# Planner with durations of the trace, fillers in any of four free banks, another front, and a table of shifts to the due dates

## The chip, the cores and the metric

The kernel runs on one core of one Trainium2 chip. What counts is the device time of one launch in microseconds (us). Before the change it is 611.71 us, the median of three runs (611.14 to 612.87).

The engines are TensorE (PE in the profile, with its weight loads as PEld), VectorE (DVE), ScalarE (ACT), GpSimd (POOL) and SyncE (SP, which only issues DMAs here). Each engine works through its own list of instructions in order. TensorE writes into eight accumulator banks, bank 0 to bank 7. In the order lists below these are called bank_63 to bank_70.

## The reference

Banded attention with a distance bias, and after it two feed-forward layers (FFN) of the same size, all in float32 with inputs of large spread:

```python
def _attn_ref(q, k, v, n_global, n_local):          # 2 x 8 heads x 768 x 64
    scores = scale * np.matmul(q, k.transpose(0, 1, 3, 2))
    is_global = pos[None, :] < int(n_global)         # 8
    is_local = (rel >= 0) & (rel < int(n_local))     # 96
    bias = -slopes[:, None, None] * dist[None, :, :]
    scores = np.where(keep, scores + bias, -1e9)
    a = np.exp(scores - np.max(scores, axis=-1, keepdims=True))
    a = a / (np.sum(a, axis=-1, keepdims=True) + 1e-09)
    return np.matmul(a, v)

def _moe_ref(x, w_in, w_out):                        # 1536 tokens, 512 -> 2048 -> 512
    h = np.maximum(x @ w_in, 0.0)
    return h * h @ w_out

def _moe2_ref(x, w_in, w_out):
    h = x @ w_in
    g = np.where(h >= 1, h, np.where(h <= -1, 0.0, (h + 1) ** 2 / 4))
    return g @ w_out
```

`reference` calls the three in this order.

## The kernel before

**Attention** is cut into 12 blocks of 128 queries (6 for each batch), and each block into two halves of four heads. One half runs through these steps: scores (TensorE, line 872, 4 or 8 products into two banks); a reduction with the mask for each head (VectorE, L894), which writes the scores plus bias back to SBUF and keeps the extreme of each row; the exponential for each head (ScalarE, L899); the sums' reciprocal (VectorE, L904 and L906); a scaling for each head (lines 155 to 159, on ScalarE, VectorE or GpSimd); transposes (TensorE, L922); a copy of the transposed part out of the bank (L131 on ScalarE or L132 on VectorE); and the products with v (TensorE, L958, "results" below). A block ends with its column of `x`, split in two float32r parts: a copy (L131 or L132) and a subtraction (L142). The masks are made once at the start, from `n_global` and `n_local`, which a small product (`broadcast_int64`, L1173) spreads over all partitions.

**Layer 0 of the FFN** is a list of 52 events (`Ffn.__init__`). An event is one 128-wide chunk of the hidden layer for 256 or 512 tokens: twelve products `h` (L537), the square of the positive part (L552 on ScalarE, L554 on VectorE), its split in two parts (L131 and L142 with output `g`), and twelve products `y` (L735) into banks 2 to 5. The first eight events are 256 tokens wide and need the first four blocks of the attention; so the attention's later blocks and the first events run between each other. Events are numbered from 0 here. An event needs the weights of its chunk in a slot: they come as raw words (`float32`, L464), ScalarE scales them (L155), VectorE puts the bits together in three passes (L472, L475, L479), and both split them into the slot's parts (L131, L142). Layer 1 works on pairs of chunks (L654 and L704).

**What sets the order.** No engine's list is written out by hand. Every operation goes to `Plan.any_of` with its engines, an assumed duration on each, a due date and the tiles that it reads and writes. `Plan.emit` then simulates the engines: whenever one is free it takes, among the operations whose inputs are ready by the assumed durations, the one that is due first, and a copy or a scaling goes to the engine of its list that would end it earlier. The program's lists are what comes out. `BEGIN`, `OTHER`, `ns_mm`, `ns_turns` and their like are the assumed times. None of them runs on the chip.

**Warm products.** The eight products of L1348 at the start multiply a tile of zeros into bank 7. Further ones, 256 columns wide, are put in where the planner sees TensorE without work for over 300 ns (`FGAP`): into bank 7 while that bank isn't used yet (L1351), later into the upper half of bank 0 (L1353), up to the first event that is 512 wide. Their results are never read.

Of the kernel before, what the change touches and what calls it, by code (L numbers as in the profile page):

```python
# [37 lines left out]
WARM, LAG = 8, 950  # L38


FGAP, BIAS = 300, 600
# [16 lines left out]
HINTED = [E.Pool, E.Activation, E.PE, E.DVE, E.SP]  # L58
BIG = 1e30
MASKED = 1e9  # L60
TOP = 3e38
P = 128
# [11 lines left out]
class Plan:  # L74
# [14 lines left out]
    def __init__(self, nc):  # L89
        self.nc = nc  # L90
        self.ops = []
        self.wrote = {}
        self.read = {}


        self.idle = []

        self.sums = {}

        self.before = {}  # L100

# [3 lines left out]
    def any_of(self, ways, due, reads=(), writes=(), lag=0, rows=P, same=SAME, tail=False):  # L105
# [5 lines left out]
        deps = set()  # L111
        writes = list(writes)
# [38 lines left out]
    def scale(self, n, due, out, in_, by, reads, writes, engines=None):  # L151
# [3 lines left out]
            ("act", ns_act(n) + (0 if isinstance(by, float) else 107), lambda: nc.scalar.activation(  # L155
# [8 lines left out]
    def emit(self):  # L164
# [35 lines left out]
        fills, idle = [], list(self.idle)  # L200
        last, open_sums, port = 0, False, 0.0
        todo = n
        while todo:
# [52 lines left out]
            if idle and i >= idle[0][2] and idle[0][1] in ops[i][5]:  # L256
                idle.pop(0)
            if engine == "pe" and idle and not open_sums:

                gap, at = t - free[engine], free[engine]  # L260
                if gap > FGAP:
                    cold = 1 + (columns.get(int(t / self.TICK) - 1, 0) < self.COLUMNS)
                    one = cold * ns_mm(256)
                    for _ in range(int((gap - 150) / one)):
                        fills.append((at, 1, idle[0][0]))
# [16 lines left out]
            free[engine] = t + ns  # L282
            todo -= 1
# [11 lines left out]
def ns_mm(n, m=P):  # L295
    return max(n, 2 * m) * 0.442 + 4


def ns_turns(n):

    return (n + 1) * 110 + 280
# [10 lines left out]
def ns_pool(n):  # L312
    return n / 0.44 + 60
# [7 lines left out]
class Ffn:  # L321
# [108 lines left out]
    def make_after(self, u):  # L430

        while self.makes and self.makes[0][1] <= u:
# [5 lines left out]
            else:  # L438
                self.make(key, i, e["due"])

# [83 lines left out]
    def h(self, u):  # L524
# [24 lines left out]
        due += 0.4 * e["len"] - G_LEAD  # L549
        bank = ("bank", kb)  # L550
# [7 lines left out]
        self.halves(N, due, r, kr, g, kg)  # L558
        self.g[u] = kg, g
# [68 lines left out]
    def pair(self, u, past):  # L628
# [12 lines left out]
        def product(kb, name, w, half, blocks, m=None, sums=True):  # L641
# [14 lines left out]
            op("pe", len(calls) * ns_mm(W), start + step[name], products, reads, [("bank", kb ^ odd)])  # L656
# [39 lines left out]
    def pair_y(self, u, n, t, due):  # L696
# [6 lines left out]
        for m, (a, b) in enumerate(MOVING):  # L703
            self.plan.op("pe", ns_mm(512), due + 0.01 * m, lambda a=a, b=b, m=m: self.nc.tensor.matmul(  # L704
# [60 lines left out]
    def leave(self, o, bank, r0, due, end):  # L765
# [690 lines left out]
```

## Time and profile before

| | before |
|---|---|
| median of the runs | 611.71 us |
| the profiled execution, its own time | 612.07 us |
| its span in the trace | 610.2 us |
| TensorE busy, share of the span | 599.0 us, 98% |
| VectorE busy | 480.0 us, 79% |
| ScalarE busy | 351.2 us, 58% |
| GpSimd busy | 60.1 us, 10% |
| granted TensorE clock, mean | 0.998 |

The span is what lies between the first and the last instruction of the program; the 1.9 us beside it are the launch's own. "Busy" counts the warm products too. The ends of the records of TensorE are modelled and reach over the next record's start, so that its steps are read from one start to the next. The records of the other engines also overlap a little with the record that follows.

### The profile page before, as it was taken

What the parts mean: (1) busy time and instruction counts of PE and PEld (TensorE: products, weight loads), DVE (VectorE), ACT (ScalarE), POOL (GpSimd) and SP (SyncE); (2) the same over time, 40 slices, a digit from 0 to 9 for tenths busy, and PEclk for the clock granted to TensorE, in tenths of its full rate; (3) what the DMA queues carried; (4) which work ended last, traced back from release to release, by engine and by line L of the source; (5) the groups of instructions that cost most, each with busy time, mean ns of one, the idle gap of its engine ahead of it and who ended that gap; (6) DMA issues with size and microseconds to landing.
All of it is one profiled execution on the core that took longest, in us unless ns stands there. A gap on an engine that the chain in (4) does not pass through costs nothing.

```text
span 610.2 us, 9671 instructions
## 1 busy us (share of the span) xinstructions
PE 599.0 (98%) x3438; PEld 513.5 (84%) x3438; DVE 480.0 (79%) x1028; ACT 351.2 (58%) x728; POOL 60.1 (10%) x88
## 2 busy tenths in 40 slices
PE   7999999999999999999999999999999999999996
PEld 5778978887888888888888898999988888999995
DVE  7999999974638987898556379999897688887863
ACT  7898877765537766564447465454543454454432
POOL 4120111010000204226200000000000000000000
PEclk9999999999999999999999999999999999999999
DMA  8553544430013879989522211323230032222002
GB/s 301 172 183 119 181 153 143 157 126 23 20 54 107 278 215 327 338 308 308 201 83 70 65 56 58 108 77 102 73 99 31 12 127 96 95 96 95 27 2 106
DMA packets 25786, 79.20 MB, mean 130 GB/s; under 512 B 2948, under 2 KB 2948, under 8 KB 25732
## 3 DMA queue, kind: packets, MB, share of 16 engines
q1 hardware_dynamic: 25730, 78.52, 38.4%
q8 instruction: 28, 0.46, 0.3%
q14 instruction: 26, 0.21, 0.1%
q10 hardware_dynamic: 2, 0.00, 0.0%
HBM read 62.78 MB, written 15.73 MB: 129 GB/s over the span
## 4 chain that ended last, share of the span: by engine, by line
PE 94%; ACT 2%; DMA 2%; DVE 1%; issue 0%; DVEq 0%; ACTq 0%
PE bank L704 22%; PE bank L735 21%; PE bank L537 21%; PE bank L654 19%; PE bank L958 3%; PE bank L922 3%; PE bank L872 3%; ACT pr L899 1%; DMA nat<-in_v_dram 1%; DMA raw<-in_moe_w_out_dram 1%; PE bank L1348 0%; PE bank L1353 0%; ACT m L155 0%; DVE x L142 0%; ACT whole L155 0%
## 5 line engine op out<-in xcount | busy, mean ns | idle before, releaser
L660 DVE TENSOR_TENSOR pr<-bank,pr 128x384 f32<-128x384 f32 x112 | 60.2, 553 | 23.8 <-PE bank L654 23.0
L142 DVE TENSOR_TENSOR g<-r,g 128x512 fp32r<-128x512 f32 (+2 forms) x74 | 49.0, 663 | 33.8 <-ACT g L131 32.8
L552 ACT ACTIVATE r<-bank 128x512 f32<-128x512 f32 (+1 forms) x52 | 29.2, 562 | 55.2 <-PE bank L537 55.0
L131 ACT ACTIVATE g<-r 128x512 fp32r<-128x512 f32 (+2 forms) x74 | 42.7, 577 | 25.3 <-DVE r L569 14.6
L899 ACT ACTIVATE pr<-pr,mn 128x256 f32<-128x256 f32 (+1 forms) x96 | 45.9, 481 | 4.4 <-DVE mn L894 4.1
L565 ACT ACTIVATE r<-pr,small 128x384 f32<-128x384 f32 x43 | 26.2, 615 | 33.9 <-DVE pr L660 33.9
L155 ACT ACTIVATE whole<-raw 128x512 f32<-128x512 f32 x52 | 34.0, 670 | 10.2 <-DMA raw<-in_moe_w_in_dram 4.0
L479 DVE SCALAR_TENSOR_TENSOR whole<-raw,whole 128x512 uint32<-128x512 uint32 x52 | 36.5, 709 | 0.4
L894 DVE CUSTOM_DVE_ANT_0 pr<-bank,m 128x256 f32<-128x256 f32 (+1 forms) x96 | 33.4, 396 | 4.3 <-PE bank L958 4.1
L475 DVE SCALAR_TENSOR_TENSOR whole<-raw,whole 128x512 uint32<-128x512 uint32 x52 | 35.4, 693 | 0.3
L159 POOL TENSOR_SCALAR pr<-pr,mn 128x256 f32<-128x256 f32 (+1 forms) x38 | 22.3, 597 | 120.0 <-DVE mn L906 56.3
L872 PEld LDWEIGHTS bank<-nat,nat 64*128 64x128 f32 x352 | 22.2, 187 | 7.6 <-issue 2.2
L567 DVE SCALAR_TENSOR_TENSOR r<-r 128x384 f32<-128x384 f32 x43 | 23.8, 556 | 5.9 <-ACT r L565 5.1
L872 PE MATMUL bank<-nat,nat 64*128 64x128 f32 x352 | 26.6, 285 | 1.7 <-DVE mn L894 1.6
L472 DVE TENSOR_SCALAR whole<-whole 128x512 uint32<-128x512 uint32 x52 | 23.5, 456 | 5.2 <-ACT whole L155 4.9
L565 ACT ACTIVATE nat<-pr,small 128x384 f32<-128x384 f32 x21 | 13.0, 617 | 25.0 <-DVE pr L660 24.9
L131 ACT ACTIVATE pr<-bank 128x512 f32<-128x512 f32 (+2 forms) x46 | 23.5, 520 | 3.9 <-PE bank L654 2.1
L958 PE MATMUL bank<-pr,nat 128*64 128x128 f32 x352 | 23.9, 277 | 1.4 <-DMA nat<-in_v_dram 0.8
L569 DVE TENSOR_TENSOR r<-pr,r 128x384 f32<-128x384 f32 x43 | 23.8, 557 | 1.2
L958 PEld LDWEIGHTS bank<-pr,nat 128*64 128x64 f32 x352 | 19.7, 136 | 5.5 <-issue 2.0
L922 PE MATMUL bank<-ident,pr 128*128 128x128 f32 x176 | 24.1, 275 | 0.0
L922 PEld LDWEIGHTS bank<-ident,pr 128*128 128x128 f32 x176 | 20.1, 140 | 3.0 <-issue 0.5
(349 smaller groups left out, 1752.3 us busy)
## 6 DMA issues: line engine op xcount, KB each, us to landing
raw<-in_moe_w_in_dram SPq DMA_DIRECT2D x32, 512.0 KB, 4.6
raw<-in_moe_w_out_dram SPq DMA_DIRECT2D x32, 512.0 KB, 4.9
whole<-sums SPq DMA_DIRECT2D x14, 512.0 KB, 3.2
kept<-whole SPq DMA_DIRECT2D x12, 512.0 KB, 6.2
whole<-kept SPq DMA_DIRECT2D x12, 512.0 KB, 3.3
whole<-kept SPq DMA_DIRECT2D x13, 384.0 KB, 2.9
sums<-pr SPq DMA_DIRECT2D x8, 512.0 KB, 6.3
nat<-in_k_dram SPq DMA_DIRECT2D x12, 256.0 KB, 3.3
```

The costliest lines, as they stand in the source:

```text
L131: ("act", ns_act(n) - 30 * psum, lambda: nc.scalar.activation(out=at(out), in_=in_, func=ACTF.Copy), False),
L142: ways = [("dve", ns_dve(n), lambda: nc.vector.tensor_tensor(out=at(out), in0=in_, in1=at(hi).bitcast(F32), op=ALU.subtract), not psum)]
L537: op("pe", ns_mm(N), due + 0.01 * m, lambda k=k, a=a, b=b, m=m: nc.tensor.matmul(out=hp, lhsT=sl[a][:, 0, k * P:(k + 1) * P], rhs=self.x[: ...
L565: op("act", ns_act(N) + 64, due, lambda: nc.scalar.activation(out=r, in_=h, func=ACTF.Relu, bias=self.half, scale=0.5), keys, [kr])
L654: nc.tensor.matmul(out=area[kb], lhsT=lhsT, rhs=at(rhs), start=(m == 0), stop=(m == len(calls) - 1))
L660: op("dve", ns_dve(W), start + step[name] + 0.2 - G_LEAD, lambda: nc.vector.tensor_tensor(out=to, in0=area[kb], in1=in1, op=ALU.add), [("b ...
L704: self.plan.op("pe", ns_mm(512), due + 0.01 * m, lambda a=a, b=b, m=m: self.nc.tensor.matmul(out=self.banks[kb], lhsT=g[:, a, cs], rhs=sel ...
L735: lambda o=o, lhsT=lhsT, rhs=rhs, n=n: nc.tensor.matmul(out=o, lhsT=lhsT, rhs=rhs, start=(e["first"] and n == 0), stop=(e["last"] and n == 2),
L872: nc.tensor.matmul(**c)
L899: op("act", ns_act(w) + 200, due, lambda e=e: nc.scalar.activation(out=pr[:, e, :w], in_=pr[:, e, :w], func=ACTF.Exp, bias=mn[:, e:e + 1], ...
L922: self.nc.tensor.transpose(self.banks[kbs[m]][:, o:o + P], pr[:, 2 * m + e, c * P:(c + 1) * P], self.ident)
L958: nc.tensor.matmul(**c)
```

## The change

It has five parts; the order in which the work goes to `Plan` is the same.

1. **Assumed times.** A product of n columns counts n / 2.4 + 13.3 ns instead of n x 0.442 + 4; groups of scores, transposes and results get formulas and lags of their own; engines begin at other times (`BEGIN`); a wait across from TensorE counts 199 ns instead of 260; a GpSimd subtraction n / 0.3 + 60 instead of n / 0.44 + 60; loads of q, k and v 1000 instead of 728.
2. **Fillers.** `idle` is now a table of four banks (7, 0, 1, 6). Where the planner sees a gap before the first wide event, it takes the bank that is clear first, by the end of the last reader of what was last written there.
3. **The front.** Five warm products at the first date and two at -9.5, instead of eight at the first. The loads of v of blocks 0 and 1 get a later date.
4. **A table `SHIFT`** of 134 numbers that are added to the due dates of whole groups: a half's scores and probabilities ("p"), its transposes and results ("r"), a block's loads ("q", "k", "v"), an event's weights ("w"), an event's square and split ("g"), and a preparation of kept weights ("prep").
5. **Output rows** that leave before the last group go out in two DMAs of 256 columns instead of one of 512.

```diff
-WARM, LAG = 8, 950
-FGAP, BIAS = 300, 600
+AGAIN = 2
+WARM, LAG = 5, 950
+FGAP, BIAS, CLEAR = 300, 600, 200
...
+SHIFT = {
+    ("g", 0): 0.83, ("g", 1): -0.13, ("g", 2): 2.01, ("g", 3): -0.22, ("g", 4): -8.66, ("g", 5): 3.04,
...
+    ("w", 9): 19.63, ("w", 10): 16.13, ("w", 11): -20.83, ("w", 28): -0.43, ("w", 29): 24.68, ("w", 30): 0.09,
...
-    OTHER = {"pe": 260, "act": 150, "dve": 130, "pool": 200}
-    BEGIN = {"act": 2000, "dma": 1680, "words": 1680, "pool": 1080, "dve": 630, "pe": 1120}
+    OTHER = {"pe": 199, "act": 150, "dve": 130, "pool": 200}
+    BEGIN = {"act": 2560, "dma": 1360, "words": 740, "pool": 1260, "dve": 980, "pe": 1390}
...
+        self.tags.append(self.tag)
+        due += SHIFT.get(self.tag, 0)
...
-            if idle and i >= idle[0][2] and idle[0][1] in ops[i][5]:
-                idle.pop(0)
-            if engine == "pe" and idle and not open_sums:
-                gap, at = t - free[engine], free[engine]
-                if gap > FGAP:
+            if engine == "pe" and not idle_end:
+                idle_end = i == self.wide
+            if engine == "pe" and idle and not idle_end and not open_sums and t - free[engine] > FGAP:
+                clear = {}
+                for bank in idle:
+                    w = wrote.get(bank)
+                    read = [u for u in users[w] if "pe" not in ops[u][0]] if w is not None else []
+                    if all(by[u] for u in read):
+                        clear[bank] = max([end[u] + CLEAR for u in read], default=0.0)
+                if clear:
+                    bank = min(clear, key=lambda b: (max(clear[b], free[engine]), -clear[b]))
+                    at = max(clear[bank], free[engine])
...
 def ns_mm(n, m=P):
-    return max(n, 2 * m) * 0.442 + 4
+    return max(n, 2 * m) / 2.4 + 13.3
 def ns_turns(n):
-    return (n + 1) * 110 + 280
+    return n * 109 + 320
+def ns_columns(n):
+    return n * 109 + 245
+def ns_transposes(n):
+    return n * 109 - 80
...
+                plan.op("dma", 364, due, lambda h=h: nc.sync.dma_start(
+                    out=self.out[r0:r0 + P, h], in_=ot[:, h]), [(*ko, n)], (), lag=LAG)
+            return
...
-            for c, lead in (("k", 3), ("q", 2.5), ("v", 2)):
+            for c, lead in (("k", 3), ("q", 2.5), ("v", 2 if blk > 1 else 0.3)):
...
-        for n in range(WARM):
-            plan.op("pe", ns_mm(512), -500 + n, lambda: nc.tensor.matmul(
+        for n in range(WARM + AGAIN):
+            plan.op("pe", ns_mm(512), -500 + n if n < WARM else -9.5, lambda: nc.tensor.matmul(
...
-        plan.idle = [[lambda: nc.tensor.matmul(
...
+        plan.idle = {("bank", kb): lambda kb=kb: nc.tensor.matmul(
+            out=banks[kb][:, 0:256], lhsT=warm[:, 0:P], rhs=warm[:, 0:256], start=True, stop=True,
+        ) for kb in (7, 0, 1, 6)}
```

Three places show what this makes of the engines' lists.

TensorE at the start, before. The product with `small` (L1173) is the broadcast of `n_global` and `n_local`; four more pairs like the first two rows stand ahead of this piece.

```order
L1348 LDWEIGHTS warm
L1348 MATMUL bank_70<-warm 128x512
L1348 LDWEIGHTS warm
L1348 MATMUL bank_70<-warm 128x512
L1173 MATMUL bank_69<-small,r_122 128x2
L1348 LDWEIGHTS warm
L1348 MATMUL bank_70<-warm 128x512
L1348 LDWEIGHTS warm
L1348 MATMUL bank_70<-warm 128x512
L872 MATMUL bank_63<-nat_125,nat_126 128x128
```

TensorE at the start, after the change (the broadcast is L1243, a warm product L1418, scores L936). One more pair like the first two rows stands ahead.

```order
L1418 LDWEIGHTS warm
L1418 MATMUL bank_70<-warm 128x512
L1418 LDWEIGHTS warm
L1418 MATMUL bank_70<-warm 128x512
L1243 MATMUL bank_69<-small,r_122 128x2
L1418 LDWEIGHTS warm
L1418 MATMUL bank_70<-warm 128x512
L1418 LDWEIGHTS warm
L1418 MATMUL bank_70<-warm 128x512
L1418 LDWEIGHTS warm
L1418 MATMUL bank_70<-warm 128x512
L936 MATMUL bank_65<-nat_125,nat_126 128x128
```

The broadcast stood behind six warm products and now stands behind three; in the first scores, those of block 0's second half are now ahead of those of its first half.

VectorE before the first event, before. L472, L475 and L479 are the three passes over a chunk's weights; `whole_118` holds chunk 0 and `whole_119` chunk 1; the subtraction into `x` ends block 1.

```order
L157 TENSOR_SCALAR pr<-pr,mn_77 128x256
L472 TENSOR_SCALAR whole_118<-whole_118 128x512 x2
L475 SCALAR_TENSOR_TENSOR whole_118<-raw_116,whole_118 128x512 x2
L479 SCALAR_TENSOR_TENSOR whole_118<-raw_116,whole_118 128x512
L472 TENSOR_SCALAR whole_119<-whole_119 128x512
L479 SCALAR_TENSOR_TENSOR whole_118<-raw_116,whole_118 128x512
L142 TENSOR_TENSOR slot0l<-whole_118,slot0h 128x512
L142 TENSOR_TENSOR x<-bank_69,x 128x4x128
L475 SCALAR_TENSOR_TENSOR whole_119<-raw_117,whole_119 128x512
```

VectorE there after the change (the passes are L527, L530 and L534, the subtractions L175, the scaling L190).

```order
L190 TENSOR_SCALAR pr<-pr,mn_77 128x256 x2
L534 SCALAR_TENSOR_TENSOR whole_119<-raw_117,whole_119 128x512
L175 TENSOR_TENSOR slot1l<-whole_119,slot1h 128x512
L527 TENSOR_SCALAR whole_118<-whole_118 128x512 x2
L530 SCALAR_TENSOR_TENSOR whole_118<-raw_116,whole_118 128x512
L175 TENSOR_TENSOR slot1l<-whole_119,slot1h 128x512
L534 SCALAR_TENSOR_TENSOR whole_118<-raw_116,whole_118 128x512
L175 TENSOR_TENSOR x<-bank_69,x 128x4x128
L530 SCALAR_TENSOR_TENSOR whole_118<-raw_116,whole_118 128x512
L175 TENSOR_TENSOR slot0l<-whole_118,slot0h 128x512
```

Chunk 1's weights are now whole before chunk 0's, and both stand ahead of the first `h`; before, chunk 1's came later.

TensorE at event 2, before: `h` is the product with `slot2`, into bank_63; the eight scores (L872) ahead of this piece belong to it too.

```order
L735 MATMUL bank_68<-g_121,slot1h 128x256
L872 MATMUL bank_69<-nat_125,nat_126 128x128
...
L958 MATMUL bank_64<-pr,nat_127 64x128 x8
L537 MATMUL bank_63<-x,slot2l 128x256
L922 MATMUL bank_69<-ident,pr 128x128 x4
L537 MATMUL bank_63<-x,slot2h 128x256
L922 MATMUL bank_70<-ident,pr 128x128 x4
L537 MATMUL bank_63<-x,slot2h 128x256
```

TensorE at event 2, after the change (`h` is L592, transposes L986).

```order
L592 MATMUL bank_63<-x,slot2h 128x256
L792 MATMUL bank_68<-g_121,slot1h 128x256
L792 MATMUL bank_68<-g_121,slot1l 128x256
L792 MATMUL bank_68<-g_121,slot1h 128x256
L986 MATMUL bank_69<-ident,pr 128x128 x4
L986 MATMUL bank_70<-ident,pr 128x128 x4
L592 MATMUL bank_63<-x,slot2l 128x256
L592 MATMUL bank_63<-x,slot2h 128x256 x2
```

Between event 1's last `y` and event 2's `h` there stood scores, results and transposes of two halves; now there are the transposes of one. Over the whole list before event 2's first `y`, TensorE had 64 scores, 48 transposes and 40 results, and now has 48, 32 and 32.

## Rows read from the trace of the kernel before

**Rows 1.** The page: the span, and TensorE's busy time.

```profile
span 610.2 us, 9671 instructions
PE 599.0 (98%) x3438; PEld 513.5 (84%) x3438; DVE 480.0 (79%) x1028; ACT 351.2 (58%) x728; POOL 60.1 (10%) x88
```

**Rows 2.** Stretches: length, each engine's busy us (instructions), clock, DMA share, GB/s.

```profile
0.00:20.00 20.00, 16.36 (x143) 11.66 (x145) 15.22 (x72) 15.45 (x53) 8.38 (x25) 1.00 0.69 250
20.00:60.00 40.00, 37.23 (x367) 32.17 (x366) 36.76 (x117) 33.70 (x96) 6.66 (x11) 1.00 0.53 170
60.00:180.00 120.00, 120.00 (x919) 99.70 (x918) 91.21 (x263) 78.98 (x211) 12.42 (x20) 1.00 0.33 109
605.40:610.20 4.80, 0.00 (x0) 0.00 (x0) 0.00 (x0) 0.60 (x1) 0.00 (x0) 0.81 0.31 115
```

**Rows 3.** Stretches again, warm products alone: PE, PEld, DVE.

```profile
4.80:20.00 15.20, 3.60 (x26) 2.51 (x25) 0.00 (x0) 1.00 0.75 281
20.00:60.00 40.00, 4.11 (x27) 2.38 (x27) 0.00 (x0) 1.00 0.53 170
60.00:610.20 550.20, 0.00 (x0) 0.00 (x0) 0.00 (x0) 1.00 0.37 122
```

**Rows 4.** Timeline of TensorE, first 8 us: start, us, what, [idle before, releaser].

```profile
1.47 2.74 PE L1348 MATMUL bank<-warm 128*128 128x512 bf16 x6 [1.47 <-DVE warm L1346]
4.01 0.38 PE L1173 MATMUL bank<-small,r 128*128 128x2 f32 x2
4.25 0.59 PE L1348 MATMUL bank<-warm 128*128 128x512 bf16 x2
4.77 1.16 PE L872 MATMUL bank<-nat,nat 64*128 64x128 f32 x16
7.73 0.49 PE L872 MATMUL bank<-nat,nat 64*128 64x128 f32 x4 [1.58 <-DVE mn L894]
```

**Rows 5.** Timeline of VectorE, 2 to 8 us.

```profile
2.46 0.15 DVE L1170 SCALAR_TENSOR_TENSOR small<-small,words 1x2 f32<-1x2 f32 x1
4.63 0.29 DVE L1008 TENSOR_SCALAR whole<-whole,bank 128x128 f32<-128x128 f32 x1 [2.02 <-ACT small L1175]
6.75 0.27 DVE L894 CUSTOM_DVE_ANT_0 pr<-bank,m 128x128 f32<-128x128 f32 x1
```

**Rows 6.** Chain of waits, 17 to 50 us: start, us, what.

```profile
21.45 4.72 DMA raw<-in_moe_w_out_dram
42.20 4.85 DMA nat<-in_v_dram
```

**Rows 7.** Timeline of TensorE: first `y` of events 2, 4 and 18.

```profile
45.87 0.39 PE L735 MATMUL bank<-g,slot2h 128*128 128x256 f32 x1
62.33 0.28 PE L735 MATMUL bank<-g,slot0h 128*128 128x256 f32 x1
174.37 0.39 PE L735 MATMUL bank<-g,slot1h 128*128 128x512 f32 x1
```

**Rows 8.** Steps of TensorE: timeline for 256 columns and transposes, chain for 512.

```profile
60.14 0.28 PE L537 MATMUL bank<-x,slot1l 128*128 128x256 f32 x1
60.26 0.40 PE L537 MATMUL bank<-x,slot1h 128*128 128x256 f32 x2
18.01 0.66 PE L922 MATMUL bank<-ident,pr 128*128 128x128 f32 x4
18.01 1.09 PE L922 MATMUL bank<-ident,pr 128*128 128x128 f32 x8
174.54 2.72 PE bank L735 x12
```

**Rows 9.** VectorE's groups by form, 0 to 60 us (busy, mean ns), and one timeline row.

```profile
L894 DVE CUSTOM_DVE_ANT_0 pr<-bank,m 128x256 f32<-128x256 f32 x35 | 13.1, 417 | 0.0
L132 DVE COPY pr<-bank 128x512 f32<-128x512 f32 x4 | 2.7, 684 | 0.7 <-PE bank L922 0.7
18.07 1.27 DVE L475 SCALAR_TENSOR_TENSOR whole<-raw,whole 128x512 uint32<-128x512 uint32 x2
```

More of the change, by code (lines that the diff above doesn't have):

```diff
@@ L93, in __init__ @@
         self.read = {}
-        self.idle = []
+        self.idle, self.wide = {}, 0
         self.sums = {}
         self.before = {}
+        self.tag = None
+        self.tags = []
     def op(self, engine, ns, due, fn, reads=(), writes=(), lag=0, rows=P, tail=False, port=False):
@@ L198, in stream @@
                 columns[int(t / self.TICK)] = columns.get(int(t / self.TICK), 0) + c
-        fills, idle = [], list(self.idle)
+        fills, idle, idle_end, wrote = [], self.idle, False, {}
         last, open_sums, port = 0, False, 0.0
@@ L255, in emit @@
                 continue
-            if idle and i >= idle[0][2] and idle[0][1] in ops[i][5]:
-                idle.pop(0)
-            if engine == "pe" and idle and not open_sums:
-                gap, at = t - free[engine], free[engine]
-                if gap > FGAP:
+            if engine == "pe" and not idle_end:
[10 more added lines that the diff above has]
+                    at = max(clear[bank], free[engine])
                     cold = 1 + (columns.get(int(t / self.TICK) - 1, 0) < self.COLUMNS)
                     one = cold * ns_mm(256)
-                    for _ in range(int((gap - 150) / one)):
-                        fills.append((at, 1, idle[0][0]))
+                    for _ in range(int((t - at - 150) / one)):
+                        fills.append((at, 1, idle[bank]))
                         stream(at, at + one, 256)
@@ L282, in emit @@
             free[engine] = t + ns
+            if engine == "pe":
+                for k in ops[i][5]:
+                    wrote[k] = i
             todo -= 1
@@ L312, in ns_pool @@
 def ns_pool(n):
-    return n / 0.44 + 60
+    return n / 0.3 + 60
 def ns_pool2(n):
@@ L654, in products @@
                     nc.tensor.matmul(out=area[kb], lhsT=lhsT, rhs=at(rhs), start=(m == 0), stop=(m == len(calls) - 1))
-            op("pe", len(calls) * ns_mm(W), start + step[name], products, reads, [("bank", kb ^ odd)])
+            op("pe", len(calls) * ns_mm(W) + 13, start + step[name], products, reads, [("bank", kb ^ odd)], lag=24)
         def add(name, kb, in1, k1, to, key):
@@ L874, in scores @@
         op("pe", ns_turns(len(calls)), due, products, [("q", rq, 0)] + [("k", rk, 0) for rk in self.rings(blk)],
-           [("bank", kb) for kb in kbs], rows=64)
+           [("bank", kb) for kb in kbs], lag=-97, rows=64)
     def probabilities(self, blk, j, due):
@@ L923, in transposes @@
                             self.banks[kbs[m]][:, o:o + P], pr[:, 2 * m + e, c * P:(c + 1) * P], self.ident)
-        self.plan.op("pe", 2 * nk * len(ms) * 108 + 80, due, transposes, [("pr", n % 3, 2 * m + e) for m in ms for e in range(2)],
-                     [("bank", kbs[m]) for m in ms], rows=64)
+        self.plan.op("pe", ns_transposes(2 * nk * len(ms)), due, transposes,
+                     [("pr", n % 3, 2 * m + e) for m in ms for e in range(2)], [("bank", kbs[m]) for m in ms], lag=83, rows=64)
         w = 2 * nk * P
@@ L958, in products @@
                 nc.tensor.matmul(**c)
-        op("pe", ns_turns(len(calls)), due, products, reads, [("bank", kb)], rows=P)
+        op("pe", ns_columns(len(calls)), due, products, reads, [("bank", kb)], lag=-98, rows=P)
         if 1 in js:
@@ L1162, in broadcast_int64 @@
     nc.vector.memset(ones, 1.0)
-    for n, (way, queue, src) in enumerate(zip(("words", "dma"), (nc.scalar, nc.sync), srcs)):
-        plan.op(way, 475, -300, lambda n=n, queue=queue, src=src: queue.dma_start(
+    for n, (way, ns, lag, queue, src) in enumerate((
+            ("words", 475, 775, nc.scalar, srcs[0]), ("dma", 50, 580, nc.sync, srcs[1]))):
+        plan.op(way, ns, -300, lambda n=n, queue=queue, src=src: queue.dma_start(
             out=words[0:1, 2 * n:2 * n + 2], in_=src.bitcast(I32).rearrange("(o n) -> o n", o=1),
-        ), (), [("words", n)], lag=960)
+        ), (), [("words", n)], lag=lag)
     low, high, r = words[0:1, 0:4:2], words[0:1, 1:4:2], one[0:1, 0:2]
@@ L1367 @@
             at.finish()
-            plan.idle[0][2] = len(plan.ops)
             at.use_banks([(6, 7)], [6, 7], [1], False)
```

27 lines of the change are left out of this document (19 added, 8 removed), and 21 rows, old and new, of the table SHIFT.

## The prediction

> **What bounds the kernel now.** I read the page first. TensorE is busy for 98% of the span [rows 1], so the time is TensorE's work, what is put between it, and what it waits. The stretches tell where the last two lie: from 60 us on TensorE is busy without a gap to the last product at 605.4, and the 4.8 us behind it hold copies and stores; in the first 60 us it is idle for 3.6 and 2.8 us [rows 2], and 3.60 and 4.11 us more are warm products between 4.8 and 60 us, none later [rows 3]. So only the front can give time back. The tail can't: the two order lists of TensorE agree from their ends back over more than a thousand products.
>
> In the front VectorE is the engine that TensorE waits for. Between 20 and 60 us it is busy for 36.8 of 40 us and ScalarE for 33.7 [rows 2]. The first gap ends on VectorE's reductions [rows 4]. The chain of waits runs twice through a DMA of 4.7 to 4.9 us, for an event's raw weights and for a block of v [rows 6].
>
> To measure how far TensorE lags I subtract its useful work from the clock at a landmark. Its steps: 0.40 - 0.28 = 0.12 us for 256 columns, 2.72 / 12 = 0.227 us for 512, (1.09 - 0.66) / 4 = 0.108 us for a score, transpose or result [rows 8]. Event 2's first `y` comes at 45.87, event 4's at 62.33, event 18's at 174.37 [rows 7]. Ahead of them the order lists hold:
> - event 2: 152 attention calls and 60 products of 256, 16.4 + 7.2 = 23.6 us of work, so a **lag** of 22.3;
> - event 4: 208 and 120, 22.5 + 14.4 = 36.9, lag 25.4;
> - event 18: 528 calls, 192 of 256, 264 of 512, 57.0 + 23.0 + 59.9 = 139.9, lag 34.5.
>
> From event 4 to 18 nothing waits, and the lag still grows by 9.1 us. TensorE changes 68 times between one kind of work and another there, so a change of kind costs 9.1 / 68 = 0.13 us.
>
> **The change, part by part.** *The broadcast.* It stands behind six warm products, runs at 4.01, and VectorE waits 2.02 us for it [rows 4, 5]. The six start at 1.47 and take (4.01 - 1.47) / 6 = 0.42 us each. Behind three it could start at 1.47 + 1.27 = 2.74; its inputs are ready at 2.46 + 0.15 = 2.61 [rows 5]. That is 1.27 us earlier, and the masks and the first reduction, now at 6.75, move with it, to about 5.5, still behind the first scores at 4.77 [rows 4, 5]. I take 1.2. Bounds: 0, if the scores' loads turn out to end the wait instead; 1.27.
>
> *VectorE's order.* I compare its lists up to event 2's split. After the change six reductions of 256 (0.34 each), three copies out of banks, a subtraction into `x` and a weight pass (0.60 each), three scalings and four small operations no longer stand ahead of it: 2.0 + 3.0 + 1.0 = 6.0 us. The steps are the records less the 0.08 by which one covers the next: two passes, about as long as the copy's record of 0.68, span 1.27 [rows 9]. The 1.0 for the last seven is an estimate: each is shorter than a reduction, which would make 2.4, and the small ones much shorter. Up to event 0 the sign is the other way: three more reductions' worth of work stands ahead, since chunk 1's weights come before chunk 0's, and the first `h` comes no earlier. Up to event 4 only 1.7 us are left; the rest was moved behind, where VectorE has 120 - 91 = 29 us free between 60 and 180 [rows 2].
>
> If VectorE waits as long on its way as before, event 2's `y` starts at 45.87 - 1.2 - 6.0 = 38.7. Ahead of it TensorE now has 112 calls and 60 products, 12.1 + 7.2 = 19.3. The lag is 19.4 instead of 22.3: **-2.9**.
>
> *From event 2 to event 4.* Before, 62.33 - 45.87 = 16.5 us hold 13.3 of work; of the 3.2 us that remain, 12 changes of kind cost 1.6, and 1.6 are waits and warm products, half of it the wait that ends with the load of v [rows 6]. After, 15.8 us of work (80 calls, 60 products: 8.6 + 7.2) and 21 changes of kind, 2.7; that v load is now issued in the first batch, so I put 0.3 for waits (bounds 0 and 1.6). Lag growth 3.0 against 3.2: **-0.1**, the smaller end of the rounding.
>
> *Behind event 4.* 68 changes of kind before and after: **0**. Eleven copies go from VectorE to ScalarE in all; at no more than VectorE's 0.68 each [rows 9] that is 7.5 us, and ScalarE has 41 us free in 60 to 180 [rows 2]. If that cover were gone, an event's split would come late, 0.6 us at a time.
>
> *Fillers.* They only fill what the planner sees as waiting: 51 of 256 columns instead of 52, but 46 ahead of the first `h` (31 before) and 5 behind it (21). A filler that isn't needed costs 0.11 us, half a 512 step; fifteen more ahead of `h` are covered by the wait for VectorE there. Bounds 0 and 1.6; I take 0. *Half stores*: six more DMA issues on SP, near 480 us, with nothing urgent queued behind; 0.
>
> The sum is -2.9 - 0.1 = **-3.0 us**. The profiled execution's own 612.07 (span 610.2 and 1.9 around it) stands 0.36 over the median; from the median, 611.71 - 3.0 = **608.7**.
>
> **The rivals.**
>
> *More comes back (606.7).* VectorE's waits between the first reduction and event 2 shrink too, because the durations that order its list are now nearer to the trace. If 2 us of what it idles there went, the gain would be 5.0. For it: both engines' idle time in 20 to 60 us is 3.2 and 6.3 us [rows 2]. Against it: a list as tight as this swaps one wait for another.
>
> *Only the broadcast counts (610.4).* ScalarE gets copies, and up to event 4 it carries about what it did; if it ends the wait in VectorE's place, of the 2.9 only the 1.2 and a little stay. For it: its 33.7 of 40 us [rows 2]. The gain is 1.3, within what a measurement can tell from no change, which is about 0.3% or 1.8 us.
>
> [...]
>
> *Slower (613.7).* SP's list. Event 2's raw weights now stand behind a small v load that waits for block 1's results, and behind a full v load; chunk 3's stand ahead. ScalarE takes them before event 1's positive part. Before, this very path held the kernel: 21.45 plus 4.72 [rows 6]. By the sums above block 1's results end near 21 us, the weights land near 27, and event 1's square wants ScalarE at about 29. Each microsecond beyond these 2 us is TensorE's. For 613.7 they would have to land 7 us late, or a second such wait follow at event 3. [...]
>
> **How the numbers follow.** The forecast of 608.7 has 0.55, the fuller gain 0.15, only the broadcast 0.20, the clock 0.04, slower 0.06. Faster by over 0.3% (under 609.9) is the first two, 0.70; within 0.3% 0.24; slower 0.06. The range's low end takes VectorE's waits down by 2.2 and the 0.3 away: 608.7 - 2.5 = 606.2. Its high end loses the 1.2 of the broadcast and has waits of 1.6 instead of 0.3: 608.7 + 2.5 = 611.2. That leaves out the slower case, the clock's and a little of the fuller gain.
>
> **What would show it.** In the new trace the broadcast product starts at 2.7 to 2.9 and the first reduction near 5.5; event 2's first `y` near 38.7 and event 4's near 57.6 to 59; TensorE is busy without a gap from there on, and the last product ends near 602.4. Warm products between 20 and 60 us take under 2 us. If the broadcast is early and event 2 isn't, VectorE or ScalarE waits for something that I took as covered, and the row of that wait names it. If event 4 is early and the end is not, a stretch behind it has new gaps. I am wrong altogether if TensorE shows waits for raw weights in events 2 and 3, or a granted clock below 1.0 in the first 60 us.

## The result and the profile after

The changed kernel takes 606.96 us against 612.15 for the kernel before beside it, a ratio of 0.991 (95% interval 0.9897 to 0.9923). A second series gave 0.992 (0.9907 to 0.9934). That is 4.9 to 5.5 us where 3.0 were forecast: the sign was right, the size too small by about two fifths. The profiled execution has 606.72 us, 5.35 under that of before. One execution of the run with more work on VectorE took 3371 us and is left out of every figure.

The page, against [rows 1], then the stretches, against [rows 2], and the warm products alone, against [rows 3] (PE, PEld, DVE):

```profile
span 604.8 us, 9664 instructions
PE 596.9 (99%) x3436; PEld 512.2 (85%) x3436; DVE 476.5 (79%) x1025; ACT 354.6 (59%) x738; POOL 50.3 (8%) x81
```

```profile
0.00:20.00 20.00, 17.00 (x141) 11.44 (x142) 15.71 (x72) 15.97 (x53) 9.14 (x26) 1.00 0.78 270
20.00:60.00 40.00, 39.58 (x400) 35.67 (x400) 37.77 (x118) 37.67 (x105) 6.22 (x11) 1.00 0.58 187
60.00:180.00 120.00, 120.00 (x910) 99.49 (x907) 88.49 (x262) 81.16 (x215) 8.50 (x16) 1.00 0.31 100
```

```profile
4.80:20.00 15.20, 4.61 (x29) 2.73 (x30) 0.00 (x0) 1.00 0.87 307
20.00:60.00 40.00, 3.37 (x23) 2.08 (x23) 0.00 (x0) 1.00 0.58 187
```

Between 20 and 60 us TensorE was idle for 2.8 us, now for 0.4. VectorE and ScalarE are both full there, ScalarE with 37.7 instead of 33.7 us. The timelines that answer [rows 4, 5, 7], of TensorE, of VectorE, and of TensorE at the three landmarks:

```profile
1.47 1.46 PE L1418 MATMUL bank<-warm 128*128 128x512 bf16 x3 [1.47 <-DVE warm L1416]
2.73 0.53 PE L1243 MATMUL bank<-small,r 128*128 128x2 f32 x2
5.38 0.72 PE L936 MATMUL bank<-nat,nat 64*128 64x128 f32 x8 [0.83 <-DMA nat<-in_k_dram]
```

```profile
3.49 0.29 DVE L1077 TENSOR_SCALAR whole<-whole,bank 128x128 f32<-128x128 f32 x1 [0.88 <-ACT small L1245]
6.22 0.29 DVE L958 CUSTOM_DVE_ANT_0 pr<-bank,m 128x128 f32<-128x128 f32 x1 [0.33 <-PE bank L936]
```

```profile
37.47 0.38 PE L792 MATMUL bank<-g,slot2h 128*128 128x256 f32 x1
55.91 0.28 PE L792 MATMUL bank<-g,slot0h 128*128 128x256 f32 x1
169.27 0.39 PE L792 MATMUL bank<-g,slot1h 128*128 128x512 f32 x1
```

Event 2 comes 8.4 us earlier, event 4 6.4, event 18 5.1, the last product 5.0 (its end at 600.35 instead of 605.37). By the prediction's steps the lag is 18.2 us at event 2 (22.3 before), 20.8 at event 4 (25.4), 29.4 at event 18 (34.5). So 4.1 of the 5 us are gained by event 2, 0.5 more by event 4 and 0.5 more by event 18. The other 4.3 us by which event 2 is earlier are no gain: they are the work of 40 attention calls that the new list moves behind it.

### The profile page after: what moved, and what is told of

It is laid out like the page before. It is cut to its first block, busy times and chain, and to the rows that moved or that the text cites. A ratio compares the mean times of both kernels' runs of the same rounds, so it can differ in the third digit from the quotient of the medians.

```text
span 604.8 us, 9664 instructions
## 1 busy us (share of the span) xinstructions
PE 596.9 (99%) x3436; PEld 512.2 (85%) x3436; DVE 476.5 (79%) x1025; ACT 354.6 (59%) x738; POOL 50.3 (8%) x81
## 3 DMA queue, kind: packets, MB, share of 16 engines
q1 hardware_dynamic: 26594, 78.52, 38.7%
## 4 chain that ended last, share of the span: by engine, by line
PE 93%; DVE 2%; DMA 2%; ACT 1%; SPq 0%; issue 0%
PE bank L761 22%; PE bank L792 22%; PE bank L592 21%; PE bank L711 20%; PE bank L1022 3%; PE bank L936 3%; PE bank L986 3%; DMA raw<-in_moe_w_out_dram 1%; DMA nat<-in_v_dram 1%; ACT pr L963 1%; DVE whole L534 0%; DVE pr L958 0%; SPq L908 0%; DVE x L175 0%; DVE slot1l L175 0%
## 5 line engine op out<-in xcount | busy, mean ns | idle before, releaser
L175 DVE TENSOR_TENSOR g<-r,g 128x512 fp32r<-128x512 f32 (+2 forms) x74 | 46.8, 632 | 43.0 <-ACT g L164 42.8
L530 DVE SCALAR_TENSOR_TENSOR whole<-raw,whole 128x512 uint32<-128x512 uint32 x52 | 37.1, 721 | 0.6
L534 DVE SCALAR_TENSOR_TENSOR whole<-raw,whole 128x512 uint32<-128x512 uint32 x52 | 36.8, 711 | 0.4
L164 ACT ACTIVATE pr<-bank 128x512 f32<-128x512 f32 (+2 forms) x56 | 28.8, 535 | 5.9 <-PE bank L986 3.9
L192 POOL TENSOR_SCALAR pr<-pr,mn 128x256 f32<-128x256 f32 (+1 forms) x36 | 19.2, 540 | 119.8 <-DVE mn L970 57.2
L936 PEld LDWEIGHTS bank<-nat,nat 64*128 64x128 f32 x352 | 22.0, 187 | 7.7 <-issue 4.4
L936 PE MATMUL bank<-nat,nat 64*128 64x128 f32 x352 | 26.5, 286 | 1.2 <-DMA nat<-in_k_dram 0.8
L527 DVE TENSOR_SCALAR whole<-whole 128x512 uint32<-128x512 uint32 x52 | 23.1, 454 | 3.7 <-ACT whole L188 3.3
L986 PE MATMUL bank<-ident,pr 128*128 128x128 f32 x176 | 24.9, 275 | 0.5 <-ACT pr L164 0.3
L986 PEld LDWEIGHTS bank<-ident,pr 128*128 128x128 f32 x176 | 20.2, 140 | 4.1 <-POOL pr L192 1.1
```

The lines of the kernel that those rows point to most:

```text
L164: ("act", ns_act(n) - 30 * psum, lambda: nc.scalar.activation(out=at(out), in_=in_, func=ACTF.Copy), False),
L175: ways = [("dve", ns_dve(n), lambda: nc.vector.tensor_tensor(out=at(out), in0=in_, in1=at(hi).bitcast(F32), op=ALU.subtract), not psum)]
L936: nc.tensor.matmul(**c)
L986: self.nc.tensor.transpose(self.banks[kbs[m]][:, o:o + P], pr[:, 2 * m + e, c * P:(c + 1) * P], self.ident)
```

## The experiments

Times are given as the ratio to the kernel before beside each run; the whole change has 0.991 and 0.992. 0.001 is 0.6 us. Landmarks are from each run's timeline of TensorE, one profiled execution each. In the old lists five such traces have the first `h` at 21.46 to 21.72; in the new ones two traces of the same kernel differ by 0.6 us there (24.64 and 25.25), so that smaller differences between landmarks say little.

**The broadcast alone.** Kernel before, the broadcast behind three warm products:

```diff
-warm x6, broadcast, warm x2
+warm x3, broadcast, warm x5
```

> The kernel before, every list as it was, with one instruction moved: the broadcast stands behind three warm products instead of six. Theory 1 (the broadcast's worth passes through VectorE's list undiminished, as the prediction took it): the broadcast starts at 2.7 to 2.9 instead of 4.01, the first reduction near 5.5 instead of 6.75, event 2's first y at 44.7 instead of 45.87, and the time is 1.2 us under the kernel before. Theory 2 (a later wait of VectorE takes the place of the one removed): the first reduction is early all the same, but event 2's first y stays within 0.4 us of 45.87, a wait behind the masks has grown by about 1 us, and the time is within 0.4 us of the kernel before.

Ratio 0.9994 (0.998 to 1.0008). The broadcast starts at 2.72, but the first reduction only at 6.71 and event 2 at 45.62. Neither expectation: the first reduction itself was hardly earlier, and the first scores, which it reads, came later:

```profile
5.33 1.80 PE L879 MATMUL bank<-nat,nat 64*128 64x128 f32 x16
```

They start at 5.33 instead of 4.77 and take 1.80 us where [rows 4] has 1.16 for sixteen. The warm products behind the broadcast were still on the longer step (five in 2.29 us, where [rows 4] has two in 0.59).

**The broadcast back, in the new lists.**

```diff
-warm x3, broadcast, warm x3
+warm x6, broadcast
```

> The changed kernel with the broadcast back behind six warm products, every list else as it is. The trace of the changed kernel has its first reduction at 6.22, only 0.53 us earlier than before, though the broadcast came 1.28 us earlier. Theory 1 (what the first reduction loses is what the kernel loses): the broadcast starts near 4.0, the first reduction at 6.7 to 7.4, and event 2's first y and the time are later by the same 0.5 to 1.2 us. Theory 2 (the early list has slack behind it): the first reduction is later, event 2's first y is within 0.3 us of 37.47 and the time within 0.3 us of the changed kernel.

Ratio 0.9942 (0.9929 to 0.9955), so 1 to 2 us are lost: first reduction at 6.95, event 2 at 38.75. That is nearer to theory 1, but more than its 0.5 to 1.2. In this trace TensorE's granted clock also fell to 0.50 between 8 and 11 us, behind a wait of 1.28 us:

```profile
7.66 3.78 PE L943 MATMUL bank<-nat,nat 64*128 64x128 f32 x32 [1.28 <-DVE mn L965]
```

The loss does not follow the clock, though: the two executions with a mean granted clock of 1.0 took 609.3 and 609.4 us, the three with 0.996 to 0.999 took 608.0 to 608.5. What the rest of the loss comes from stays open.

**No fillers.** What the prediction calls the clock is the case that TensorE's granted clock falls where fillers are gone. Here the 51 warm products of 256 columns are left out of the changed kernel:

```diff
-        calls = [(start[i], 0, ops[i][0][by[i]][1]) for i in order] + fills
+        calls = [(start[i], 0, ops[i][0][by[i]][1]) for i in order]
```

> The changed kernel without the 51 warm products of 256 columns that fill the planned waits (their results are not read); the lists are else as they are, and the seven of 512 stay. The prediction's step (fillers are covered by waits, cost nothing and aren't needed for the clock): the time is within 0.4 us of the changed kernel, the granted clock stays 1.0. The clock rival: the granted clock of a stretch between 5 and 30 us is under 1.0 and the first events' products take the longer step, 24 of them 0.12 us each, so about 2.9 us more. Needless fillers: up to 5 x 0.11 = 0.6 us less, and event 2's first y earlier by as much.

Ratio 0.9934 (0.9922 to 0.9947), 0.9 to 1.5 us lost, and every execution has a mean granted clock of 0.995 to 0.997, where those of the changed kernel have 0.998 to 1.0. The stretch where it falls:

```profile
14.00:17.00 3.00, 3.00 (x18) 1.81 (x18) 2.47 (x12) 2.56 (x11) 1.31 (x3) 0.56 0.74 264
```

In the 3 us ahead of it TensorE was busy for 1.86 us only, against 2.62 in the first trace of the changed kernel, whose granted clock is 1.00 in both stretches. The first `h` comes at 26.02 instead of 24.64 or 25.25. So the fall that the clock rival expects is there without the fillers, for about half or less of its 2.9 us; with them it isn't.

**No table.**

```diff
-SHIFT = {
-    ("g", 0): 0.83, ("g", 1): -0.13, ("g", 2): 2.01, ("g", 3): -0.22, ("g", 4): -8.66, ("g", 5): 3.04,
...
+SHIFT = {}
```

> The changed kernel with an empty table of shifts: the new durations, front, fillers and half stores stay. Its lists have 35.4 us of VectorE's work up to event 2's split (32.9 with the table, 39.0 before the change, by the same records), 50.4 up to event 4's (48.6 and 50.0), and TensorE has 137 attention calls ahead of event 2's y (113 and 153) and 97 changes of kind in all (85 and 95). Theory 1 (VectorE's list is what counts, and the table sets it): event 2's first y comes about 2.5 us later than with the table, at 40 to 42, event 4's at 60 to 61, and the time is 3 us over the changed kernel, about 1.5 to 2 under the kernel before. Theory 2 (the durations and the front bring the gain, the table is a detail): within 1 us of the changed kernel.

Ratio 0.9984 (0.997 to 0.9998): of the gain of 5 us, 1 is left. Theory 1: event 2 came as written, event 4 0.15 us later, and 4 us are lost where 3 were expected:

```profile
42.00 0.40 PE L767 MATMUL bank<-g,slot2h 128*128 128x256 f32 x2
61.15 0.28 PE L767 MATMUL bank<-g,slot0h 128*128 128x256 f32 x1
```

VectorE's waits did not shrink with the new durations. Those over 0.15 us that its timeline lists up to event 2's split, without the one for the broadcast, sum to 3.9 us before, 4.4 without the table, and 3.3 and 3.8 in two traces of the changed kernel.

The table changes every engine's list, TensorE's too, so this run doesn't single out VectorE's. Event 2's `y` less VectorE's work ahead of it (the counts in the expectation) is 6.9 us before, 6.6 without the table and 4.6 with it; less TensorE's own work, by the prediction's steps, it is 22.3, 20.1 and 18.2. VectorE's list follows the date more closely, but not fully.

**More work on one engine ahead of event 2.** One operation on event 2's weights is done four times instead of once, on VectorE (the subtraction into the low part) or on ScalarE (the copy into the high part):

```diff
+            calls[at:at] = 3 * [calls[at]]
```

> The changed kernel with one VectorE pass of event 2's weights (slot 2, low part, near 33.1) done four times instead of once: 3 x 0.60 = 1.8 us more on VectorE ahead of event 2's split, the result the same, all other lists as they are. Theory 1 (VectorE's list still sets when event 2's y starts, and nothing behind gives it back): event 2's first y near 39.2 instead of 37.47, event 18's and the last product later by the same 1.8, the time 1.8 over the changed kernel. Theory 2 (from the first h on TensorE's own work is now as long as VectorE's list, it is busy 39.6 of 40 us between 20 and 60): event 2's y moves by under 0.9, or event 4's takes the loss back, and the time rises by under 0.6.

> The changed kernel with one ScalarE copy of event 2's weights (slot 2, high part, near 31.5) done four times instead of once: 3 x 0.52 = 1.6 us more on ScalarE ahead of event 2's positive part, the result the same, all other lists as they are. Theory 1 (VectorE alone sets event 2): ScalarE's list swallows it, event 2's first y within 0.5 of 37.47, the time within 0.5 us of the changed kernel. Theory 2 (the prediction's rival that ScalarE has taken VectorE's place, busy 37.7 of 40 us between 20 and 60): event 2's y and the time later by 1.6.

VectorE: ratio 0.9977 (0.9967 to 0.9987), 4 us lost for 1.8 added. ScalarE: 0.9958 (0.9945 to 0.9971), 2.5 lost for 1.6. TensorE's rows for event 2's `h`, of the first and of the second, and a stretch of the first:

```profile
36.70 0.41 PE L596 MATMUL bank<-x,slot2l 128*128 128x256 f32 x1 [2.18 <-DVE slot2l L175]
```

```profile
34.97 0.39 PE L596 MATMUL bank<-x,slot2h 128*128 128x256 f32 x1 [1.67 <-ACT slot2h L164]
```

```profile
38.00:40.00 2.00, 2.00 (x14) 1.78 (x15) 1.23 (x4) 1.23 (x4) 1.47 (x2) 0.50 0.70 262
```

Each engine's extra work became a wait of TensorE in full, so both now set event 2; "VectorE alone" falls. After the wait of 2.18 us the granted clock went to 0.50 as well, and event 2's first `y` came at 41.83: a delay of 1.8 us cost twice its length. From the `h` at 36.70 to that `y` are 5.13 us, where the changed kernel, from this row to 37.47, has 3.62:

```profile
33.85 0.39 PE L592 MATMUL bank<-x,slot2l 128*128 128x256 f32 x1
```

The other executions agree: nine with a mean granted clock of 0.995 to 0.997 took 610.7 to 611.7 us, the two with 0.999 and 1.0 took 608.28 and 609.81, so that without the fall the loss was 1 to 3 us. In the run with more work on ScalarE the clock stayed at 1.00 after the wait of 1.67 us and the loss stayed near the wait; four of its five executions took 609.1 to 609.4 us with a mean of 1.0, one 610.67 with 0.997.

**Short loads of raw weights.** Kernel before, two transfers bring one eighth:

```diff
+            wide = 64 if layer == 0 and c == 2 and self.plan.idle else 512
```

> The kernel before, every list as it was, but two transfers made short: the raw weights of chunk 2 in layer 1, issued at 20.01 and 21.45, bring 64 of 512 numbers of each half, so that event 2 computes with stale weights; all instructions that read them stay. ScalarE waited 1.37 and 0.88 us for these two, and VectorE after that 1.03 and 0.22 us at 31.55 and 32.46. Theory 1 (these waits are the part of the lag that the prediction took as unchanged, and that the change also removed): VectorE's waits near 31 to 33 fall under 0.4 us in sum, event 2's first y comes 0.9 to 1.7 us earlier than 45.87, at 44.2 to 45.0, and the time falls by as much. Theory 2 (VectorE finds another wait behind them): event 2's y within 0.4 us of 45.87 and the time within 0.4 us of the kernel before.

Ratio 0.9993 (0.9985 to 1.0002), event 2 at 45.76: the raw weights were not what VectorE waited for, although ScalarE's two waits for them are gone from its timeline. VectorE's row is the same as before:

```profile
31.44 0.43 DVE L555 SCALAR_TENSOR_TENSOR r<-bank,r 128x256 f32<-128x256 f32 x1 [1.04 <-PE bank L1354]
```

Line 1354 is a filler. That is the step that I had passed over. The kernel before has at this place, on TensorE and on VectorE:

```profile
30.85 0.60 PE L1353 MATMUL bank<-warm 128*128 128x256 bf16 x4 [0.47 <-ACT r L552]
32.03 0.38 PE L1353 MATMUL bank<-warm 128*128 128x256 bf16 x2 [0.59 <-DVE r L554]
```

```profile
31.55 0.43 DVE L554 SCALAR_TENSOR_TENSOR r<-bank,r 128x256 f32<-128x256 f32 x1 [1.03 <-PE bank L1353]
```

These fillers write bank 0 while event 1's `h` in bank 0 has been read by ScalarE but not by VectorE. They wait for the one reader, and the other waits for them. VectorE is idle from 30.52; 0.3 of its 1.03 us pass before the four fillers start at 30.85, the other 0.7 while they run.

**The filling rule alone.** Kernel before with the changed choice of banks: same instructions, same order, six fillers behind event 2's `h` left out, four of them just ahead of its first `y`.

```diff
-                        fills.append((at, 1, idle[0][0]))
+                        fills.append((at, 1, idle[bank]))
```

> The kernel before with the new filling rule alone: the same instructions in the same order, but the 256-column warm products go into banks whose readers are done (6, 7, 0, 1) instead of bank 7 and then bank 0, and six of them, behind event 2, are left out. Before, seven fillers stand in bank 0, event 1's own, between ScalarE's read of it and VectorE's: four at 30.85 wait 0.47 us for ScalarE, VectorE's read at 31.55 waits 1.03 us for them, and two at 32.03 wait 0.59 us for VectorE. Theory 1 (the filler holds VectorE up, and that is the part of the wait that the prediction took as staying): the waits of 1.03 and 0.22 go, event 2's first y comes 0.9 to 1.3 us before 45.87, and the time falls by 0.9 to 1.3 us. Theory 2 (VectorE's next wait takes it back): event 2's y within 0.4 us of 45.87, the time within 0.4 us of the kernel before.

The waits are gone and event 2's `y` starts at 44.86, as theory 1 says, and event 4's at 60.08; the profiled execution has 609.93 us, 2.1 less. VectorE's row now:

```profile
30.64 0.42 DVE L564 SCALAR_TENSOR_TENSOR r<-bank,r 128x256 f32<-128x256 f32 x1
```

The time isn't settled: ratio 0.9988 (0.9972 to 1.0005). Of its twelve executions seven, with a mean granted clock of 0.998 or more, took 609.7 to 611.5 us, and five with 0.994 to 0.997 took 611.7 to 614.5. No trace of one of those five was taken, so where the clock fell in them stays open.

**The old banks in the new lists.** The changed kernel, only the fillers' banks as before.

```diff
-                        fills.append((at, 1, idle[bank]))
+                        fills.append((at, 1, idle[0][0]))
```

> The changed kernel with the old filling rule: the same instructions in the same order on every engine, only the banks of the 51 fillers are the old ones (bank 7, from the first event on bank 0). Theory 1 (a filler in a bank that is still to be read holds its reader): the front is later by 0.5 to 1.5 us, seen first in a wait of VectorE or ScalarE that ends with a warm product between 8 and 32 us, and event 2's y and the time are later by as much. Theory 2 (the new list leaves few fillers behind the first h, so the bank no longer matters): within 0.4 us of the changed kernel.

Ratio 0.9921 (0.9907 to 0.9934), no other than the changed kernel's; the medians, each of its own series, are 608.0 us against 607.0 and 607.2. The first `y` comes 5.2 us behind the first `h` instead of 4.7, behind this row:

```profile
28.18 0.43 DVE L603 SCALAR_TENSOR_TENSOR r<-bank,r 128x256 f32<-128x256 f32 x1 [0.34 <-PE bank L1416]
```

The mechanism is there in the new lists too, for some 0.4 us between the first `h` and event 2's `y` (13.3 us instead of 12.8). In the time it can't be told from nothing, so that neither theory is settled.

**Front and filling rule together, old lists.** Both edits in the kernel before.

```diff
-warm x6, broadcast, warm x2
+warm x3, broadcast, warm x5
...
-                        fills.append((at, 1, idle[0][0]))
+                        fills.append((at, 1, idle[bank]))
```

> The kernel before with two parts of the change at once, the broadcast behind three warm products and the new filling rule; VectorE's, ScalarE's, GpSimd's and SyncE's lists are those of before. Alone, the filling rule brought event 2's first y from 45.87 to 44.86 and event 4's from 62.33 to 60.08, the broadcast 45.62 and 61.52. Theory 1 (the parts add, and what is then left to the changed kernel's 37.47 and 55.91 is the lists' own): event 2's y at 43.6 to 44.7, event 4's at 59 to 59.9, the profiled execution 2.3 to 3.3 us under the kernel before's 612.07, with the granted clock at 1.0. Theory 2 (the parts hide each other, or the list was never what counted): event 2's y at 44.8 or later, or so early (under 42) that the lists have little left to explain.

Ratio 0.9974 (0.9959 to 0.999), 1.6 us; event 2 at 45.46, event 4 at 60.85.

```profile
31.25 0.42 DVE L571 SCALAR_TENSOR_TENSOR r<-bank,r 128x256 f32<-128x256 f32 x1 [0.58 <-ACT r L569]
```

In the landmarks the two do not add up, and event 2 falls in theory 2's range: where the filler is out of the way, VectorE waits 0.58 us for ScalarE instead. In the same trace ScalarE had waited 1.66 us, until 26.74, for event 2's raw weights (0.88 before, 0.73 with the filling rule alone). So once the filler is gone this load can be on the path; the short loads showed it off the path only with the filler in its place. In the time, 0.4 and 0.7 us alone and 1.6 together can't be told from a sum.

What lies between this kernel and the changed one, 3.3 to 4 us of time, is the order of the lists, and about 0.4 at the end with the half stores. At event 2 the two are 8.0 us apart, 4.3 of which are the calls that were moved behind it.

**The changed kernel again, and with four more warm products.** The first has no edit, the second:

```diff
-warm x3, broadcast, warm x3
+warm x3, broadcast, warm x7
```

> The changed kernel once more, nothing edited. Three runs whose lists equal its up to the first h (the 1.8 us more on VectorE, the 1.6 us more on ScalarE, the old filling rule) had that first h at 25.31 to 25.47, the changed kernel's trace at 24.64. Theory 1 (the front's date moves by some tenths from one execution to the next, with the loads): the first h anywhere from 24.6 to 25.5, event 2's y 12.8 us behind it, as in the first trace, the granted clock 1.0 throughout, the time 606.2 to 608. Theory 2 (the three edits reached back and delayed the first h themselves): the first h within 0.2 us of 24.64.

> The changed kernel with four more warm products of 512 columns (their results aren't read) right behind the broadcast, seven there instead of three; everything else as it is. In its second trace, and in those of the three edits of its front, the warm products behind the broadcast and the first 48 scores still take the longer step: 8 scores 1.22 us and the next 40 4.5 us, where its first trace has 0.72 and about 3.3, and the first h comes at 25.25 to 25.47 instead of 24.64. Theory 1 (in the new front TensorE mostly still runs at its low level there, and that costs the first h about 0.6 us): with seven in a row the level rises before or soon after the scores, 8 scores take about 0.72 us, and although they start up to 1.3 us later the first h comes at 24.5 to 25.2; the time is up to 0.6 us under the changed kernel. Theory 2 (VectorE's masks and reductions set the first h, the scores' step doesn't matter): the first h follows the later scores, at 25.5 to 26.5, and the time is 0.3 to 1.2 us over it.

The second trace has its first `h` at 25.25 and event 2 at 38.08, 12.8 us behind it, as theory 1 says; ratio 0.992. What differs between the two traces of this kernel is TensorE's step at the start. Its rows in the second trace, and with seven warm products behind the broadcast:

```profile
4.67 1.22 PE L936 MATMUL bank<-nat,nat 64*128 64x128 f32 x8
6.37 4.52 PE L936 MATMUL bank<-nat,nat 64*128 64x128 f32 x40
```

```profile
6.04 0.71 PE L941 MATMUL bank<-nat,nat 64*128 64x128 f32 x8
24.77 0.38 PE L597 MATMUL bank<-x,slot0h 128*128 128x256 f32 x1
```

With seven the scores start 1.4 us later and yet the first `h` comes 0.5 us earlier, so the step does count, by one trace of each. In the time it can't be seen: ratio 0.9921 (0.9899 to 0.9942).

## Why the prediction came out as it did

*Bound and lever: right in the main.* The front gave nearly all of the time back, the order of the lists made most of it, and what event 2 gained lasted to the end. Without the table 4 of the 5 us are gone; with the broadcast and the filling rule but the old lists 1.6 are there. That it is VectorE's list in particular is in part argued: no run changes one engine's list alone, TensorE's own order changed with it, and in the new lists ScalarE binds as much as VectorE.

The sum's terms as dates, against the two traces of the changed kernel (the columns add up, with the 1.9 us around the span and to 0.1, to each execution's own time; 609.07 is 612.07 less 3.0):

| | forecast | first trace | second trace |
|---|---|---|---|
| event 2's first `y` | 38.7 | 37.47 | 38.08 |
| from there to event 4's | 15.8 + 2.7 + 0.3 = 18.8 | 18.44 | 18.57 |
| to the end of the last product | 543.04 + 16 x 0.108 = 544.77 | 544.44 | 544.45 |
| to the end of the span | 4.8 | 4.41 | 4.37 |
| own time | 609.07 | 606.72 | 607.41 |

So 0.6 to 1.2 us of what was missed lie ahead of event 2, and three terms that I had put at nothing or nearly so give 0.2 to 0.4 each.

*Broadcast, -1.2: right start, wrong use.* It started at 2.73 as worked out, and VectorE's work behind it at 3.49 instead of 4.63. But the first reduction came at 6.22 (6.02 in the second trace), not at 5.5. One mask more stands ahead, and in the first trace the first scores came at 5.38 and held it for 0.33 us, which was the bound of 0 that I had named. In the old lists the broadcast alone is worth at most 1.2 us and most likely 0.4; put back in the new ones it costs 1 to 2.

*VectorE's list, -6.0: a little short in work and in waits.* From its first work behind the broadcast to event 2's split VectorE took 41.22 us before, 33.89 and 34.48 in the two traces of the changed kernel, and was busy for 38.15, 31.74 and 31.80 of them. So its work fell by 6.4 us, and its idle time, 3.1 before, by 0.9 or 0.4. The step that failed is "if VectorE waits as long on its way as before". The rival "more comes back" gave 606.7 us, nearer to what came out than the forecast, but that is partly luck, since its reason failed: durations nearer to the trace did not shorten the waits, and without the table VectorE idles 3.5 us on this way. With the table it idles less, for the list that the table was made for, and well under the 2 us that the rival took.

*Event 2 to 4, and behind event 4.* Twenty-one changes of kind at 0.13 us leave nothing of the 0.3 for waits, and from event 4 to event 18 the 112.04 us became 113.36 with 1.73 us more work in them, so 0.4 less. I had put the changes of kind there as equal.

*Fillers, 0: the term that was wrong in kind.* I priced a filler by its length alone. Its bank was what cost: in the old lists the rule takes 2.2 us off event 4's date and 2.1 us off the profiled execution, though the ratio over all executions, 0.9988, does not settle it. Between events 2 and 4 three traces with the old rule have 16.46, 15.90 and 16.08 us, two with the new one 15.22 and 15.39. Not all of that is the filler's: in the 16.46 the wait that ends with the load of v is 0.81 us, which the other traces have at 0 to 0.43. In the new lists, which have few fillers behind the first `h`, the rule is worth some 0.4 us in the trace and nothing clear in the time.

*Half stores, 0.* The span ends 4.35 to 4.5 us behind the last product in all nine traces with half stores, and 4.8 in all five without. No run isolates them.

*The clock, 0.04.* The rows of before show the granted clock at 1.00 up to 180 us [rows 2], so this chance was an estimate of mine. The changed kernel's stayed at 1.00 in the same stretches, as forecast. But without fillers it fell to 0.56, and with 1.8 us more on VectorE to 0.50, which went with a loss of 0.9 to 1.5 us and of some 2 beyond the 1.8 added. The 2.9 us for 24 products, 0.12 each, no run shows: they were an estimate from the step of 256 columns [rows 8].

*Slower, by raw weights: not seen.* Event 2's raw weights, issued at 23.14 and 25.36, landed at 27.30 and 28.55, near the 27 of the prediction, and ScalarE took them at 27.70 and 29.25 without a listed wait. Its one wait for raw weights there, 0.89 us at 24.40 in the first trace, is for the load issued at 19.31, by the prediction's order event 3's; the second trace has none. That the old waits of 1.37 and 0.88 us held the kernel, as the prediction says, was wrong: the short loads took them away, and nothing came of it while the filler stood behind them.

## What to carry to other kernels

Filler work can hold another engine, here VectorE for a wait of 1.03 us: put it where no reader of its bank is still to come, and look in the trace for waits that end with it. When an order list is changed, count its work, but don't carry its old waits over; find out for each large wait what releases it: here VectorE's row named a filler, and I had taken the raw weights that ScalarE waits for nearby as the cause. In this list, with both helper engines full, there was no slack: 1.6 to 1.8 us more on either cost 2.5 to 4 us.

## What the runs showed of the hardware

- At the start TensorE took 0.42 us for 512 columns [rows 4], later 2.72 / 12 = 0.227 [rows 8], though the granted-clock column shows 1.00 from 1.5 to 3 us too. With six warm products ahead of the broadcast and two behind it, these two, from 4.25 on, took 0.52 us from start to start; with three ahead and five behind, the five took 2.22 us, until 5.33. In the changed kernel's second trace the first 48 scores, until 10.8 us, were still on the longer step (eight in 1.22 us, 40 in 4.52). In its first trace, with the same instructions, eight scores at 5.38 took 0.72 us. With seven warm products behind the broadcast, eight scores at 6.04 took 0.71. What decides between the two in the same program stays open.
- The granted clock fell after a wait of 2.18 us that ended at 36.7 (0.50 from 38 to 40 us) and not after one of 1.67 us that ended at 34.97; but it also fell after one of 1.28 us that ended at 7.66, with the broadcast put back, and not after one of 1.58 us in the kernel before [rows 4]. Each is one trace, and the length of the wait alone doesn't tell.
- Fillers in event 1's bank held VectorE's read of that bank in the kernel before: VectorE was idle for 1.03 us, 0.7 of them from the start of the four products on. With the fillers in other banks no such wait is listed.
